# Row loads, one-hot global rows and eight-block units in a fused attention and feed-forward kernel

## The chip, the cores and the metric

The kernel runs on one core of one Trainium2 chip. The time of a run is the device time of that core in microseconds (us). A kernel is compared with another by runs taken on the same chip. The profiled span is a little shorter than the time of the same run (378.6 us of 380.3 before the change).

## The reference, cut to what matters

Eight batches of 576 tokens go through windowed attention with eight global tokens, and the 4,608 resulting rows of 512 go through a feed-forward layer with a snake activation.

```python
# attention: B=8, H=8, S=576, D=64; float32 inputs
mask = (abs(i - j) <= 32) | is_global[i] | is_global[j]
attn = softmax(where(mask, q @ k.T / sqrt(D), -1e9))
x = (attn @ v)            # to (B*S, H*D) = (4608, 512)
# feed-forward
h = x @ w_in              # (4608, 2048)
g = h + sin(alpha * h) ** 2 / (alpha + 1e-9)
out = g @ w_out           # (4608, 512), float32
```

The mask is sparse: a block of 48 queries sees 112 keys of its window and the 8 global keys. The 8 global query rows see every key; their sums are gathered over all blocks and written into their places at the end of a batch.

## The kernel before

The engines are PE (matmul), DVE and ACT (elementwise), POOL (elementwise, and the issuer of most loads) and SP (the issuer of plain copies and of the output). The order of instructions on each engine is the order in which the program is written. One batch of attention fills 576 columns of `xT`, and then one chunk of 512 tokens goes through the first matmul (`hb <- xT, w_in`). The second matmul of that chunk (`ops` and `o <- w_out, H2b`) is mixed into the next batch's attention. So PE runs a rhythm: a stretch of `hb` matmuls, then attention with second matmuls, then `hb` again. I call the time from one first `hb` matmul to the next a phase. The first matmul of a chunk is written in 16 steps of four `hb` matmuls, called slots (0 to 15); work of other kinds can be written between two of them.

The parts that the change touches:

```python
setup = tc.alloc_tile_pool(name="setup", bufs=1)
...
# q, k in tiles of 96 tokens; one DMA per head (batches 0, 1) or per tile (others)
QS = qkp.tile([TW, NTW, H, D], BF, name="QS")      # 96 x 6 x 8 x 64
...
# all 64 global rows of k, q, v, gathered at the start into tiles of their own
gN = [setup.tile([NG * B, DM], F32, name=f"gN{i}") for i in range(3)]
...                                                # registers loaded on SP and ACT
for i, src in enumerate((k, q, v)):
    for eng, js in halves:                         # half on SP, half on ACT
        for j in js:
            eng.dma_start(out=gN[i][j : NG * B : NG, :]..., in_=src[:, :, bass.ds(regs[j], 1), :]...)
nc.scalar.dma_start(out=alphaT[:], in_=moe_alpha.rearrange("(t p) -> p t", p=P))
...
def stage_T(b, hp, qpool, qtag):                   # 6 transposes of two heads each, for k and for q
    for jt in range(NTW):
        nc.tensor.transpose(out=Kps[:, WIN + jt * TW : ...], in_=KS[:, jt, 2 * hp : 2 * hp + 2, :], ...)
    nc.vector.tensor_copy(out=kTw[hp][:, :, 0:KB], in_=<overlapping windows of Kps>)
...
def stage_Q(psA, b, hp, hf):                       # one unit: 6 blocks
    ...                                            # 12 score matmuls
    nc.scalar.activation(out=E[:], in_=Sp[:, :, 0:EW], func=AF.Exp, scale=scale)
    nc.vector.tensor_tensor(out=E[:], in0=E[:], in1=mk..., op=ALU.mult)
...
def stage_V(psA, b, hp, hf, E, rec, gn):
    ...                                            # 12 matmuls num <- E, VW
    nc.vector.tensor_tensor(out=xT[:, hp, x0 : x0 + NU * QB]..., in0=num[:, :, 0:QB], in1=rec[:], op=ALU.mult)
...
def stage_G(b, gn, gr):                            # POOL scatters the global rows into xT
    for j in range(NG):
        nc.gpsimd.tensor_copy(out=xT[:, :, b * S : (b + 1) * S][:, :, bass.ds(pregs[j], 1)],
                              in_=xg[:, :, j : j + 1])
...
if p == 0:
    stage_T(0, 0, psA, "qp"); globals_all(); ...; globals_v_all()
    shift_v(0); global_v(0)                        # copies within the v buffer; global v rows into it
    parts, last = attention(0, psA, {2: 0, 3: 2})
    with_extra(parts, w_loads, 3, 2)               # 8 weight loads, two per part of the attention
    parts[3] = partial(chain, parts[3], pool_regs) # POOL loads 8 registers for the scatter
    late = load_slots(1, True)                     # batch 1 is loaded during chunk 0
```

The softmax here doesn't subtract the row's maximum and nothing guards it: scores larger than these inputs give would overflow.

## Time and profile before

| | before |
|---|---|
| time, median of 3 runs | 380.93 us (380.72 to 382.26) |
| profiled span | 378.6 us |
| first `hb` matmul | 46.60 us |
| first phase, second phase | 43.5 us, 38.1 us |
| each of the next five phases | 38.0 us |
| last `hb` start of a phase to the end | 60.4 us |

The page of the kernel before shows the span in 40 slices of 9.5 us; each digit is the busy share of a slice in tenths (`PEclk` is the granted TensorE clock in tenths):

```profile
span 378.6 us, 8594 instructions
...
PE   1127499698999999999999999999999999999996
...
DVE  7735459574987487748774877487748774866510
...
PEclk9999999999999999999999999999999999999999
DMA  6999999546999428951896289628962001000112
```

From slice 6 on PE is at 9 nearly everywhere. The opening, slices 1 to 5, is where PE has little to do, and there the DMA row is near full. `PEclk` reads 9 throughout, but the durations of the first `hb` matmuls say otherwise. The view of the line (shortest, median and longest duration in ns) shows those that ran between 46.6 and 49.6 us, and those between 50 and 52 us:

```profile
L457 PE MATMUL hb<-xT,w_in x7: 444/634/634, 46.6 to 49.5; 128*128 128x512 bf16 x7
...
L457 PE MATMUL hb<-xT,w_in x11: 379/379/380, 49.8 to 52.0; 128*128 128x512 bf16 x11
```

The first ones take 634 ns, the later ones 379. By these durations the kernel before starts its feed-forward at about half clock; its first eight `hb` matmuls (one of them is missing from the records) take 3.2 us.

The timeline of PE has start, duration, engine, line, operation and count, and in brackets what ended the idle time before:

```profile
29.58 0.57 PE L375 MATMUL num<-E,VW 128*64 128x56 bf16 x12 [3.08 <-DMA VW<-VgN]
...
46.60 0.59 PE L457 MATMUL hb<-xT,w_in 128*128 128x512 bf16 x1 [3.35 <-POOL xT L402]
```

The first product with v waited for the gathered global v rows until 29.58 us; the feed-forward started at 46.60 us, released by POOL's scatter into `xT`.

Two DMA views, 8 to 20 us and then 36 to 48 us, show what POOL's queue moved: packets, MB written, share of 16 engines.

```profile
q0 software_dynamic: 8487, 1.06, 139.0%
```

```profile
q0 software_dynamic: 2342, 2.32, 121.1%
```

In the first stretch the rows of q, k, v are 256 bytes, and 1.06 MB in 12 us is 88 GB/s; in the second the weights come in rows of 2 KB, and 2.32 MB in 12 us is 193 GB/s (bytes as written, in bf16), though the engines were no busier. The Trainium skill ("DMA: Bandwidth & Descriptors", Specifications) says that line rate needs transfers of at least 512 bytes; these two stretches agree with that.

The windows of the first three phases (columns named in the first line; busy us, with the number of instructions):

```profile
core 0: us, PE busy (x) PEld busy (x) DVE busy (x) ACT busy (x) POOL busy (x), PEclk, DMA share, GB/s
46.60:90.10 43.50, 37.92 (x378) 18.42 (x385) 28.59 (x73) 32.83 (x57) 23.85 (x44) 1.00 1.09 103
90.10:128.20 38.10, 36.95 (x378) 18.10 (x384) 26.89 (x64) 32.51 (x57) 31.40 (x53) 1.00 1.55 136
128.20:166.30 38.10, 36.38 (x379) 18.10 (x385) 26.64 (x59) 29.58 (x50) 31.24 (x48) 1.00 0.94 97
```

In the third window PE is busy for 36.38 of 38.10 us at full clock. A phase is bound by PE, and ACT or DVE time saved in it can gain little.

### The profile page before, as it was taken

The page shows a single profiled execution, that of the slowest core. Times are in us where ns is not written, and L with a number is a line of the kernel's source. Part 1 is how long each engine was busy: PE and PEld are TensorE (multiplying, and loading weights), DVE is VectorE, ACT ScalarE, POOL GpSimd, SP SyncE. Part 2 cuts the span into 40 slices and gives each one's busy share as a digit, 9 for nine tenths or more (in the row PEclk, how much of TensorE's full clock was granted, in tenths as well). Part 3 has the DMA queues.
Part 4 walks back from the last instruction along what each step waited for, and adds up shares of the span by engine and source line. Part 5 has one row for each costly group of instructions (what it writes and reads, how often), then busy time and mean ns, then how long its engine had stood idle before and what let it go on. Part 6 is the DMA issues. An engine that isn't in the chain of part 4 may idle for free.

```text
span 378.6 us, 8594 instructions
## 1 busy us (share of the span) xinstructions
PE 328.3 (87%) x3173; PEld 164.0 (43%) x3224; DVE 244.5 (65%) x556; ACT 258.1 (68%) x435; POOL 245.6 (65%) x390
## 2 busy tenths in 40 slices
PE   1127499698999999999999999999999999999996
PEld 0015244343444444444444444445444544444444
DVE  7735459574987487748774877487748774866510
ACT  1056587795998588858885888588858885845411
POOL 8944297136979489948994899489948303965100
PEclk9999999999999999999999999999999999999999
DMA  6999999546999428951896289628962001000112
GB/s 52 131 167 168 192 156 162 56 51 90 156 135 164 103 40 74 164 109 45 70 165 110 47 64 167 110 51 62 169 100 58 29 32 55 2 1 28 55 57 83
DMA packets 133867, 35.31 MB, mean 93 GB/s; under 512 B 123330, under 2 KB 128450, under 8 KB 133826
## 3 DMA queue, kind: packets, MB, share of 16 engines
q0 software_dynamic: 122560, 19.02, 70.0%
q1 hardware_dynamic: 8034, 15.40, 14.1%
q10 hardware_dynamic: 3232, 0.34, 0.8%
q8 instruction: 25, 0.41, 0.5%
q14 instruction: 16, 0.13, 0.1%
HBM read 38.42 MB, written 9.44 MB: 126 GB/s over the span
## 4 chain that ended last, share of the span: by engine, by line
PE 53%; ACT 17%; POOL 10%; issue 8%; DVE 8%; DMA 2%; POOLq 1%; ACTq 0%; DVEq 0%
PE hb L457 22%; PE ops L494 12%; PE o L494 8%; ACT Sb L464 6%; ACT E L342 3%; PE num L375 3%; ACT S L470 2%; DVE H2b L447 2%; DMA KS<-in_k_dram 2%; DVE S L472 2%; DVE kTw L310 2%; PE hb L494 2%; PE Sp L336 2%; ACT lnd L358 2%; POOL QS L95 2%
## 5 line engine op out<-in xcount | busy, mean ns | idle before, releaser
L457 PE MATMUL hb<-xT,w_in 128*128 128x512 bf16 x562 | 130.7, 382 | 7.0 <-POOL xT L402 4.8
L464 ACT ACTIVATE Sb<-hb,alphaT 128x512 bf16<-128x512 f32 x144 | 96.6, 684 | 52.4 <-PE hb L457 51.1
L447 DVE SCALAR_TENSOR_TENSOR H2b<-S,recipT,hb 128x512 bf16<-128x512 bf16 x144 | 102.2, 740 | 21.0 <-POOL S L472 21.0
L472 POOL TENSOR_TENSOR S<-Sb 128x512 bf16<-128x512 bf16 x87 | 88.4, 1040 | 29.7 <-ACT Sb L464 29.5
L457 PEld LDWEIGHTS <-w_in 128*128 128x128 bf16 x576 | 56.4, 98 | 73.7 <-issue 9.5
L494 PE MATMUL ops<-w_out,H2b 128*128 128x512 bf16 x286 | 73.3, 380 | 2.3 <-issue 1.7
L494 PEld LDWEIGHTS <-H2b 128*128 128x128 bf16 x560 | 48.7, 98 | 52.6 <-issue 2.2
L344 DVE TENSOR_TENSOR E<-E,MASK 128x672 bf16<-128x672 bf16 x64 | 33.1, 519 | 32.8 <-ACT E L342 32.1
L494 PE MATMUL o<-w_out,H2b 128*128 128x512 bf16 x206 | 50.6, 379 | 2.2 <-issue 1.9
L342 ACT ACTIVATE E<-Sp 128x672 bf16<-128x672 f32 x64 | 45.9, 717 | 4.1 <-PE Sp L336 4.0
L402 POOL COPY xT<-xg 128x4 bf16 x64 | 12.9, 201 | 48.7 <-DVE xg L400 45.3
L107 POOL DMA_DIRECT2D VW<-in_v_dram x56 | 42.7, 796 | 0.4 <-issue 0.3
L358 ACT ACTIVATE lnd<-den 128x288 f32<-128x288 f32 x64 | 26.4, 412 | 17.7 <-PE den L352 17.2
L472 DVE TENSOR_TENSOR S<-Sb 128x512 bf16<-128x512 bf16 x35 | 20.4, 582 | 25.0 <-ACT Sb L464 24.1
L382 DVE TENSOR_TENSOR xT<-num,rec 128x288 bf16<-128x288 f32 x64 | 28.7, 448 | 6.8 <-PE num L375 5.4
L375 PEld LDWEIGHTS <-VW 128*64 128x64 bf16 x768 | 18.3, 116 | 32.6 <-DVE gn L386 10.2
L375 PE MATMUL num<-E,VW 128*64 128x56 bf16 x768 | 25.3, 201 | 6.6 <-DMA VW<-VgN 3.1
L360 ACT ACTIVATE rec<-lnd 128x288 f32<-128x288 f32 x64 | 28.3, 443 | 2.0
L310 DVE COPY kTw<-Kps 128x1344 bf16<-128x1344 bf16 x32 | 27.1, 848 | 1.9 <-PE Kps L304 1.9
L336 PE MATMUL Sp<-qT,kTw 64*128 64x56 bf16 x768 | 22.1, 190 | 6.0 <-ACT E L342 4.2
L100 POOL DMA_DIRECT2D QS<-in_q_dram x30 | 23.6, 786 | 2.8 <-DMA QS<-in_q_dram 2.8
L324 ACT COPY qT<-qp 128x576 bf16<-128x576 bf16 x20 | 12.6, 632 | 18.1 <-DMA gN<-in_v_dram 13.7
(77 smaller groups left out, 314.3 us busy)
## 6 DMA issues: line engine op xcount, KB each, us to landing
out_dram<-osb SPq DMA_DIRECT2D x35, 256.0 KB
VW<-in_v_dram POOLq DMA_DIRECT2D x40, 112.0 KB, 4.4
VW<-VW SPq DMA_DIRECT2D x8, 384.0 KB
KS<-in_k_dram POOLq DMA_DIRECT2D x30, 96.0 KB, 4.6
QS<-in_q_dram POOLq DMA_DIRECT2D x30, 96.0 KB, 4.6
w_in<-in_moe_w_in_dram POOLq DMA_DIRECT2D x4, 512.0 KB, 9.0
w_out<-in_moe_w_out_dram POOLq DMA_DIRECT2D x4, 512.0 KB, 13.7
VW<-VW SPq DMA_DIRECT2D x8, 240.0 KB
```

The costliest lines, as they stand in the source:

```text
L107: nc.gpsimd.dma_start(out=W[p0 : p0 + n, par, u, :].rearrange("p (h d) -> p h d", d=D), in_=v[b, :, key0 : key0 + n, :].rearrange("h p d - ...
L310: nc.vector.tensor_copy(out=kTw[hp][:, :, 0:KB], in_=bass.AP(tensor=base.tensor, offset=base.offset, ap=[list(base.ap[0]), [QB, NW], [1, KB]],
L336: nc.tensor.matmul(out=Sp[:, t, u * QC : (u + 1) * QC], lhsT=kTw[hp][pr, i, :], rhs=qT[hp][pr, i, :], start=True, stop=True, skip_group_ch ...
L342: nc.scalar.activation(out=E[:], in_=Sp[:, :, 0:EW], func=AF.Exp, scale=scale)
L344: nc.vector.tensor_tensor(out=E[:], in0=E[:], in1=mk[:, None, :].to_broadcast([P, 2, EW]), op=ALU.mult)
L358: nc.scalar.activation(out=lnd[:], in_=den[:, :, 0:QB], func=AF.Ln)
L375: nc.tensor.matmul(out=num[pr, u, :], lhsT=W[:, i % 2, i // 2, c0 : c0 + 64], rhs=E[:, t, u * QC : (u + 1) * QC], start=True, stop=True, s ...
L447: nc.vector.scalar_tensor_tensor(out=H2b[:, n_, :], in0=s_[:], scalar=recipT[:, n_ : n_ + 1], in1=h_, op0=ALU.mult, op1=ALU.add,)
L457: nc.tensor.matmul(out=h2[:], lhsT=w_in[:, ci, nt * P : (nt + 1) * P], rhs=xT[:, ci, c * CH : (c + 1) * CH], start=(ci == 0), stop=(ci == ...
L464: nc.scalar.activation(out=Sb[:], in_=h2[:], func=AF.Sin, scale=alphaT[:, nt : nt + 1])
L472: eng.tensor_tensor(out=S2[:], in0=Sb[:], in1=Sb[:], op=ALU.mult)
L494: nc.tensor.matmul(out=ops[:], lhsT=H2b[:, nt, ts * P : (ts + 1) * P], rhs=w_out[:, nt, :], start=(nt == 0), stop=(nt == NT - 1),)
```

## The change

The intent is to shorten the opening and to relieve ACT and DVE. The changed parts are these:

1. q and k of batches 0 and 1 are loaded in rows of 8 tokens (2 KB contiguous), and transposed one head and one row position at a time.
2. Batch 0's mask is added by PE as a bias (identity times a bias tile) ahead of the scores; its global q and k rows come from matmuls with a one-hot tile (zeros with a single one in each column, so that the product picks out rows), its global v rows from eight small loads. So batch 0 no longer needs the big gather.
3. The big gather (24 transfers, all on SP now, after the v copies) lands in the last columns of `xT`, which are not used until the last batches; nothing else needs it before chunk 0.
4. A unit has 8 blocks rather than 6, so a batch has 6 units rather than 8.
5. The loads of POOL are written in one run (w_in, q and k of batch 1, w_out, v of batch 1), ahead of its register loads.
6. Batch 1 is transposed during chunk 0, and its global rows are converted there; the squares of the first two chunks go to POOL, as in the later ones.

```diff
+    late_x = slice(NTOK - 2 * DM, NTOK)
+    gN = [xT[0 : NG * B, i, late_x].bitcast(F32) for i in range(3)]
+    gB = [xT[0 : NG * B, 3, NTOK - (2 - i) * DM : NTOK - (1 - i) * DM] for i in range(2)]
...
+    def rows(src, dst, h0):                       # batches 0, 1
+        nc.gpsimd.dma_start(
+            out=dst[:, h0 : h0 + H // 2].rearrange("p h j d -> p h (j d)"),
+            in_=src[b, h0 : h0 + H // 2].rearrange("h (p j) d -> p h (j d)", j=R8))
...
+    VgF = setup.tile([P, DM], F32, name="VgF")
+    VgZ = setup.tile([P, DM], BF, name="VgZ")
+    zero(VgF[96:128, :])
+    nc.vector.memset(VgZ[:].bitcast(F32), 0.0)
+    ...                                           # per row: register load, then
+            eng.dma_start(out=VgF[KB + j : KB + j + 1, :]..., in_=v[0, :, bass.ds(regs[j], 1), :]...)
+    def gather_all():
+        for j in range(NG // 2, NG):
+            regs[j] = nc.sync.value_load(gsc[0:1, 2 * j : 2 * j + 1], min_val=0, max_val=S - 1)
+        nc.sync.dma_start(out=alphaT[:], in_=moe_alpha.rearrange("(t p) -> p t", p=P))
+        for i, src in enumerate((k, q, v)):
+            for j in range(NG):
+                nc.sync.dma_start(out=gN[i][j : NG * B : NG, :]..., in_=src[:, :, bass.ds(regs[j], 1), :]...)
...
     def globals_all():
         for i in range(2):
-            nc.vector.tensor_copy(out=gB[i][:], in_=gN[i][:])
+            nc.vector.tensor_copy(out=gB[i], in_=gN[i])
...
     def stage_T(b, hp, qpool, qtag):
+        if b < 2:
+            return stage_T8(b, hp, qpool, qtag)   # 16 transposes for k, 16 for q
+        if b == 2 and hp == 0:
+            zero(Kps[:, 0:WIN].bitcast(F32))
+            zero(Kps[:, WIN + S : WIN + S + WIN].bitcast(F32))
...
+        if b == 0:
+            for t, pr in heads:
+                nc.tensor.matmul(out=Sp[:, t, 0:EW], lhsT=identb[:], rhs=BIAS[...], start=True, stop=False, ...)
...
                 if p == 0:
                     stage_T(0, 0, psA, "qp")
-                    globals_all()
+                    globals_0(0, psC, "ops")      # one-hot matmuls
...
                     shift_v(0)
-                    global_v(0)
-                    parts, last = attention(0, psA, {2: 0, 3: 2})
-                    with_extra(parts, w_loads, 3, 2)
+                    gather_all()
+                    globals_v0()
+                    zero_v(1)
+                    parts, last = attention(0, psA, {2: -1, 3: 0})
+                    early = w_loads[:4] + load_rows(1) + w_loads[4:] + v_loads(1)
+                    chain(*early)
                     parts[3] = partial(chain, parts[3], pool_regs)
...
+                if p == 0:                        # during chunk 0
+                    gin = [partial(globals_in, 1, hp) for hp in range(NHP)]
+                    m1[8] = partial(chain, m1[8], globals_all, *gin)
```

## The prediction

> **What bounds the kernel now.** Span 378.6 us. (1) Opening: the first long run of expert matmuls starts at 47.41 us (chain of waits). The slices' DMA row is near full from about 2 to 48 us: 256-byte rows of q, k, v moved about 95 GB/s (DMA view, 8 to 20 us), the weights' 2 KB rows about 200 GB/s (36 to 48 us), counted as bf16. Batch 0 waits for the gathered global v rows until 29.6 us (timeline of PE), then runs its units; POOL's scatter ends at 46.6. (2) Steady phases of 38 us each (expert matmuls start at 128.9, 166.4, 204.9, 242.4, 280.9, 318.4): PE idles only 1 to 2 us in each (windows), so ACT or DVE savings gain little.
>
> **What the change does.** q and k of batches 0, 1 move in 2 KB rows: 1.18 MB per batch takes about 6 us of DMA instead of 12. Transposes grow from 12 to 32 per head pair; the kTw copy becomes strided (0.85 us, estimate 1.4). Batch 0 loses eight mask products (0.51 us each) and the wait for gathered v, and gains twelve bias matmuls and one-hot matmuls; its scores can start near 13 us instead of 20. Six units of eight blocks replace eight of six: ACT per batch 8 x (0.72+0.41+0.44) = 12.6 us becomes about 11.8; PE columns stay equal.
>
> **Where the gain should go.** Two new waits, read from the built program's order:
> - The gather's landing buffers now lie in xT. Batch 0's first product into xT waits for the last eight gather transfers, though nothing overlaps. SP issues all 24 after the v shift: start about 15 us, 24 x 0.8 us (measured), landing near 40. Five units and the sums remain: scatter done near 54.
> - POOL issues w_in, batch 1's q, k, w_out and batch 1's v before its register loads (5.3 us in the trace) and the scatter. An issue waits for the one eight earlier, so the last waits for the third w_out load: by bytes at the measured rates 44 to 46 us; plus registers and scatter, about 54.
>
> So expert matmuls start near 54 us instead of 47.4: plus 6 to 7. Given back: batch 1 is transposed during chunk 0's matmuls, and squares leave ACT; the 42.7 us to the next phase becomes about 40.5 (DVE has some 17 us of work in chunk 0): minus 2. Steady attention stretches (22.4 to 22.9 us) lose bubbles: minus 0.6 each, six times. Sum: about plus 1.
>
> The Trainium skill ("DMA: Bandwidth & Descriptors", opening table) puts line rate at transfers of 512 B and more; this case's rates, 95 against 200 GB/s, agree.
>
> **Prediction:** 382 us, 8 in 10 between 373 and 390. Faster by over 2%: 0.18; within 2%: 0.66; slower: 0.16.
>
> **What would show each step.** q, k landing near 6 us, v near 14. Scores of batch 0 before 15. DVE's first xT product idle until about 40, released by a gather DMA. POOL's register loads after 45; expert matmuls from 52 to 57. Next phase 40 to 41 us later; phases after that 37 to 38.
>
> **What would make it wrong.** Gathers issued or landed much faster, or the loads draining by 38 us: expert matmuls then come before 47, time near 372. Or 8-block units bound by ACT (1.96 us a unit against PE's 1.8), phases grow: near 388. Or one-head transposes costing PE several us in batch 1.

## The result, and the profile after

| | before | after |
|---|---|---|
| time, median | 380.91 us (4 runs) | 409.13 us (408.86 to 409.72, 4 runs) |
| profiled span | 378.6 us | 407.9 us |
| first `hb` matmul | 46.60 us | 71.00 us |
| first phase | 43.5 us | 45.0 us |
| second phase | 38.1 us | 42.2 us |
| next five phases together | 190.0 us | 189.8 us |
| rest | 60.4 us | 59.9 us |

The ratio of the times is 1.0735, with a 95% interval from 1.0707 to 1.0763. Here and below a ratio is the mean time of one kernel's fast runs over that of the other's fast runs of the same rounds, so it is not quite the ratio of the medians quoted. The kernel is slower, and outside the predicted range. By the rows of the table, the 29.3 us of span come from the opening (+24.4), the first phase (+1.5), the second phase (+4.0), the five steady phases (-0.2) and the end (-0.5).

The same rows of the page, after the change (slices of 10.2 us):

```profile
span 407.9 us, 9090 instructions
...
PE   2272025889897999999999999999999999999996
...
DVE  8330034578647664876497469638864975584530
...
PEclk9997558889998999999999999999999999999999
DMA  9999960009940795199409934972995000100022
```

Slices 4 to 6 of PE read 2, 0 and 2, and DVE's 0, 0 and 3: a hole from about 33 to 58 us, at whose end the DMA row runs out too. `PEclk` falls to 5 in the hole and is not back at 9 until slice 10, and it dips again to 8 in slice 13, near 130 us.

PE's timeline, at the places where it waited:

```profile
58.91 0.63 PE L516 MATMUL num<-E,VW 112*64 112x56 bf16 x16 [25.89 <-DVE gd L482]
...
71.00 9.28 PE L614 MATMUL hb<-xT,w_in 128*128 128x512 bf16 x36 [3.40 <-POOL xT L561]
82.16 0.29 PE L322 MATMUL ops<-identb,xT 64*128 64x64 bf16 x4 [1.88 <-DVE xT L320]
83.33 0.29 PE L322 MATMUL ops<-identb,xT 64*128 64x64 bf16 x4 [0.89 <-DVE xT L320]
...
116.01 9.66 PE L614 MATMUL hb<-xT,w_in 128*128 128x512 bf16 x44
128.70 0.64 PE L413 MATMUL Kps<-identb,KS 96*128 96x96 bf16 x6 [3.03 <-DVE Kps L184]
```

The hole of 25.89 us ends at 58.91 and is put down to DVE. The two waits of 1.88 and 0.89 us are for casts of the gathered rows, and the 3.03 us wait is for a zeroing of `Kps`. On DVE's timeline:

```profile
57.85 0.56 DVE L545 TENSOR_TENSOR xT<-num,rec 128x384 bf16<-128x384 f32 x1 [27.64 <-DMA xT<-in_v_dram]
...
81.52 1.75 DVE L320 CAST xT<-xT 64x512 bf16<-64x512 f32 x2
...
128.42 0.22 DVE L184 MEMSET Kps<- 128x16 f32 x2
```

DVE's first product into `xT`, ready since about 30 us, sat 27.64 us until a DMA into `xT` released it. The transfer named, `xT<-in_v_dram`, is one of the gathers; batch 0 writes the first 576 columns of `xT`, the gathers the last 1,024. Nothing overlaps. The prediction had read this wait from the built program's order.

SP issues the gathers. Its timeline shows what it did when; the view by line gives shortest, median and longest duration of the issues in ns:

```profile
10.22 7.54 SPq L296 DMA_DIRECT2D VgF<-in_v_dram  x4
18.02 0.57 SPq L140 DMA_DIRECT2D VW<-VW  x1
...
22.39 0.44 SPq L309 DMA_DIRECT2D alphaT<-in_moe_alpha_dram  x1
23.05 16.19 SPq L312 DMA_DIRECT2D xT<-in_k_dram  x8
39.43 6.72 SPq L312 DMA_DIRECT2D xT<-in_q_dram  x8
46.34 6.68 SPq L312 DMA_DIRECT2D xT<-in_v_dram  x8
```

```profile
L312 SPq DMA_DIRECT2D xT<-in_k_dram x8: 592/596/6982, 23.1 to 38.6; - x8
```

SP's one-row v loads (`VgF`) began at 10.22 us, after DVE had zeroed their tile, and ended at 17.76. The v copies went out at 18.02 and 18.65, four register loads took until 22.39, and then came the load of alpha. The k gathers right behind it took 16.19 us for eight issues, against 6.72 and 6.68 us for the q and v gathers. The issue right behind the alpha load took 6,982 ns, where their median is 596. The last k gather (38.65 us) came just after alpha's landing, at 22.39 + 16.24 = 38.63 us, as the chain of waits shows. In the kernel before, alpha came behind ACT's gathers, at 16.42 us, and held only a reciprocal on DVE. The chain:

```profile
22.39 16.24 DMA alphaT<-in_moe_alpha_dram
...
52.42 4.81 DMA xT<-in_v_dram
...
71.00 3.25 PE hb L614 x8
...
116.15 9.52 PE hb L614 x44
```

The second line of that chain is the last gather, issued at about 52.4 us and landed 4.8 us later. After the release at 57.85 us it took 13.2 us to the first `hb` matmul at 71.00. Those first eight took 3.25 us, 406 ns each; the 44 of the next phase took 9.52 us, 216 ns each.

POOL's scatter shows that POOL was not what held the opening, since it waited 20.36 us for DVE:

```profile
68.91 2.03 POOL L561 COPY xT<-xg 128x4 bf16 x8 [20.36 <-DVE xg L559]
```

Last, five windows after the change, with the columns as in the windows of before (the clock is the column after POOL's):

```profile
33.00:58.00 25.00, 0.01 (x2) 0.00 (x0) 0.15 (x1) 0.64 (x1) 5.38 (x7) 0.56 1.30 145
63.50:70.00 6.50, 2.76 (x77) 1.61 (x77) 3.63 (x14) 4.64 (x7) 0.85 (x5) 1.00 0.02 4
71.00:74.30 3.30, 3.30 (x10) 1.20 (x10) 0.00 (x0) 0.72 (x2) 0.63 (x1) 0.58 0.00 0
128.70:133.80 5.10, 5.10 (x37) 2.88 (x37) 2.52 (x4) 2.27 (x4) 1.40 (x2) 0.70 0.00 0
158.20:196.20 38.00, 36.67 (x382) 17.99 (x381) 26.10 (x51) 28.74 (x44) 30.94 (x48) 1.00 0.94 97
```

PE was granted 0.56 of its clock in the hole, 1.00 again from 63.5 to 70.0 us, 0.58 over the first `hb` matmuls, and 0.70 after the 3.03 us wait. So the low clock of the first `hb` matmuls came with the 3.40 us wait for the scatter just before them, not with the long hole. The Trainium skill ("TensorE: Matmul & The Clock Gate", "Why this matters for your kernels") warns of idle gaps beyond some 3 us, after which the clock is halved, and Part 1 gives 3.4 us of work before it is full again. Both agree: 406 ns a matmul after 3.40 us of waiting and 216 ns later, and the lower clock after 3.03 us of waiting. The eight slow matmuls are no loss against the kernel before, which has them too. The steady phase in the last line is no shorter than before (PE 36.67 us busy).

### The profile page after: what moved, and what is told of

Same layout as the page of the kernel before. It is cut to its first block, busy times and chain, and to the rows that moved or that the text cites. A ratio compares the mean times of both kernels' runs of the same rounds, so it can differ in the third digit from the quotient of the medians.

```text
span 407.9 us, 9090 instructions
## 1 busy us (share of the span) xinstructions
PE 340.5 (83%) x3508; PEld 168.6 (41%) x3508; DVE 238.3 (58%) x483; ACT 245.8 (60%) x373; POOL 250.7 (61%) x384
## 3 DMA queue, kind: packets, MB, share of 16 engines
q1 hardware_dynamic: 10922, 15.52, 14.4%
## 4 chain that ended last, share of the span: by engine, by line
PE 59%; ACT 12%; DMA 9%; DVE 8%; issue 5%; POOL 4%; SPq 2%; POOLq 0%; ACTq 0%; DVEq 0%
PE hb L614 26%; PE ops L651 12%; PE o L651 10%; DMA alphaT<-in_moe_alpha_dram 4%; ACT E L470 4%; PE num L516 3%; ACT Sb L621 3%; DVE S L629 2%; DVE H2b L604 2%; DVE kTw L419 2%; PE Sp L464 2%; ACT L578 2%; DMA w_in<-in_moe_w_in_dram 2%; DMA xT<-in_q_dram 2%; PE hb L651 2%
## 5 line engine op out<-in xcount | busy, mean ns | idle before, releaser
L629 POOL TENSOR_TENSOR S<-Sb 128x512 bf16<-128x512 bf16 x113 | 115.0, 1041 | 43.3 <-ACT Sb L621 42.9
L503 ACT ACTIVATE lnd<-den 128x384 f32<-128x384 f32 x48 | 23.5, 490 | 48.1 <-PE den L497 48.1
L561 POOL COPY xT<-xg 128x4 bf16 x64 | 12.9, 201 | 60.2 <-DVE xg L559 56.8
L470 ACT ACTIVATE E<-Sp 128x896 bf16<-128x896 f32 x48 | 43.6, 909 | 6.9 <-PE Sp L464 6.7
L516 PE MATMUL num<-E,VW 120*64 120x56 bf16 (+1 forms) x768 | 21.6, 198 | 27.2 <-DVE gd L482 25.9
L474 DVE TENSOR_TENSOR E<-E,MASK 128x896 bf16<-128x896 bf16 x42 | 26.4, 628 | 26.8 <-ACT E L470 26.7
L545 DVE TENSOR_TENSOR xT<-num,rec 128x384 bf16<-128x384 f32 x32 | 17.7, 554 | 30.7 <-DMA xT<-in_v_dram 27.6
L516 PEld LDWEIGHTS <-VW 120*64 120x64 bf16 (+1 forms) x768 | 16.5, 114 | 45.9 <-issue 38.5
L131 POOL DMA_DIRECT2D KS<-in_k_dram x36 | 28.2, 783 | 0.0
L505 ACT ACTIVATE rec<-lnd 128x384 f32<-128x384 f32 x48 | 25.1, 523 | 1.5
L629 DVE TENSOR_TENSOR S<-Sb 128x512 bf16<-128x512 bf16 x23 | 16.2, 703 | 16.1 <-ACT Sb L621 15.9
L464 PEld LDWEIGHTS <-kTw 64*128 64x128 bf16 x768 | 15.4, 95 | 23.2 <-issue 17.0
```

Source lines behind the costliest of these rows:

```text
L131: nc.gpsimd.dma_start(out=dst[:, t, :, :], in_=src[b, :, t * TW : (t + 1) * TW, :].rearrange("h p d -> p h d"),)
L464: nc.tensor.matmul(out=Sp[:, t, m * QC : (m + 1) * QC], lhsT=kTw[hp][pr, i, :], rhs=qT[hp][pr, i, :], start=b > 0, stop=True, skip_group_c ...
L474: nc.vector.tensor_tensor(out=E[:], in0=E[:], in1=mk[:, None, :].to_broadcast([P, 2, EW]), op=ALU.mult)
L505: nc.scalar.activation(out=rec[:], in_=lnd[:], func=AF.Exp, scale=-1.0)
L516: nc.tensor.matmul(out=num[pr, m, :], lhsT=W[0:nk, i % 2, i // 2, c0 : c0 + 64], rhs=E[0:nk, t, m * QC : (m + 1) * QC], start=b > 0 or m = ...
L629: eng.tensor_tensor(out=S2[:], in0=Sb[:], in1=Sb[:], op=ALU.mult)
```

## The experiments

The working theory, A, was that the time goes to the landing place: the gathers into `xT` hold DVE, and their lateness (alpha first, then register loads, one queue) sets how long. Rival B was that POOL's order of loads holds the start (its last v issue was at 48.03 us, and the register loads and the scatter stand behind it). Rival C was that the change makes PE's own work in the first two phases costlier, by transposes and the masks, whenever the start is. The runs were made on four chips; each ratio is to the kernel before on the same chip. All the outputs were correct. Every experiment is the changed kernel with the edits shown or named; from e9_mendv on, each builds on the one before it (e12_actcast on e10_best).

### e1_land: another landing place, all else the same

```diff
+    hpool = ctx.enter_context(tc.tile_pool(name="hpool", bufs=2))
-    gN = [xT[0 : NG * B, i, late_x].bitcast(F32) for i in range(3)]
+    gl = hpool.tile([P, NT, CH], BF, name="H2b")[0 : NG * B].rearrange("p t c -> p (t c)")
+    gN = [gl[:, 2 * i * DM : 2 * (i + 1) * DM].bitcast(F32) for i in range(3)]
```
(and `gB` likewise; the pool that holds H2b is made earlier)

> The changed kernel with the landing buffers of the global rows moved out of xT, into a buffer of H2b that stands free until later; nothing else moved. Theory A (batch 0's first product into xT waits for the gathers only because they land in xT): that product no longer waits for a DMA and runs near 30 us instead of 57.9; POOL's scatter is then held by POOL's own order (last v load of batch 1 issued near 48.6, register loads of 5.3 us): first expert matmul near 56 to 57 us instead of 71.0, time 393 to 396. Rival B (POOL's queue of DMA issues is what holds the scatter): no change, 408 to 410. Rival C (more transposes and a slower PE clock cost the time): at most 3 us gained.

Measured: 393.62 us, ratio 1.0305 [1.0284, 1.0325]. DVE's first product into `xT` in this run, and POOL's scatter:

```profile
30.19 0.56 DVE L546 TENSOR_TENSOR xT<-num,rec 128x384 bf16<-128x384 f32 x1 [0.17 <-PE num L527]
```

```profile
53.08 2.05 POOL L562 COPY xT<-xg 128x4 bf16 x8 [4.88 <-issue]
```

The product came at 30.19 us with the gathers as late as before; the wait of 27.64 us is gone, so the landing place made it. The start of `hb` moved from 71.00 only to 55.17 us, since now POOL's register loads (the 4.88 us ahead of the scatter, "issue") and the scatter behind the last v load set it. That is the second wait that the prediction named, at 55.17 for a predicted 54; after the change it was hidden behind the first one.

### e2_alpha: alpha's load early, on ACT's queue

```diff
     nc.scalar.dma_start(out=gcol[KB : KB + NG, :], in_=global_idx[:, None])
+    nc.scalar.dma_start(out=alphaT[:], in_=moe_alpha.rearrange("(t p) -> p t", p=P))
...
-        nc.sync.dma_start(out=alphaT[:], in_=moe_alpha.rearrange("(t p) -> p t", p=P))
```

> The changed kernel with only the load of alpha moved from SP, where the gathers queue behind it, to the front of ACT's queue. Theory A with its detail (eight gathers later the semaphore of the slow 4-byte-element load of alpha comes round, so the k gathers take 16.2 us instead of 6.2): the gathers land near 48 instead of 57.6, first expert matmul near 61, time 398 to 401. If the gathers are slow in themselves because the loads crowd the DMA engines: under 3 us gained.

Measured: 402.91 us, ratio 1.0525 [1.0502, 1.0547]. SP's gathers of k and q, and DVE's first product:

```profile
22.48 6.25 SPq L312 DMA_DIRECT2D xT<-in_k_dram  x8
28.91 9.23 SPq L312 DMA_DIRECT2D xT<-in_q_dram  x8
```

```profile
50.88 0.56 DVE L545 TENSOR_TENSOR xT<-num,rec 128x384 bf16<-128x384 f32 x1 [20.69 <-DMA xT<-in_v_dram]
```

The k gathers took 6.25 us in place of 16.19, so the alpha load cost 9.9 us there. DVE was released at 50.88, 7.0 us earlier, and `hb` started at 64.07, 6.9 us earlier. The start was expected near 61. The q gathers now took 9.23 us rather than 6.72: SP waited for slots among the k gathers instead, 2.7 us in five waits. And the last gather, issued at 43.78 us, released DVE 7.1 us later, where it had been 5.4. The packets of the alpha load can be counted: between the two pages, the queue of SP (q1) loses 2,064 packets (10,922 to 8,858) and another one (q10) gains 2,064 (368 to 2,432).

### e3_pool: POOL's order, all else the same

```diff
-                    early = w_loads[:4] + load_rows(1) + w_loads[4:] + v_loads(1)
+                    early = w_loads[:4] + load_rows(1) + [pool_regs] + w_loads[4:]
-                    parts[3] = partial(chain, parts[3], pool_regs)
...
+                    with_extra(m1, v_loads(1), 0, 1)     # during chunk 0
```

> The changed kernel with only POOL's order mended: register loads before the w_out loads, batch 1's v loads after the scatter, one behind each slot of chunk 0's matmuls. Theory A: the wait for the gathers still ends last, first expert matmul within 1.5 us of 71, time 407 to 411 (a little more if the later v loads delay POOL's squares or the shift of v). Rival B: first expert matmul at 50 to 57 us, time 390 to 396.

Measured: 410.86 us, ratio 1.0744 [1.0725, 1.0762], no gain in time. The start of `hb` was at 68.50, 2.5 us earlier and a little outside the 1.5 us expected, since DVE was released at 55.05 instead of 57.85. The first phase more than gave it back: 49.7 us rather than 45.0, with a wait of PE of 6.43 us for the casts of the gathered rows. POOL was free 33.88 us before the scatter and waited for DVE. So POOL's order was not what held the start in the changed kernel.

### e4_landpool: e1 and e3 together

> Both edits together (landing buffers out of xT, and POOL's order). Theory A with POOL's order as the second wait behind it: units of batch 0 run from 30 us, scatter near 43, first expert matmul near 44 us, but the global rows still land near 57 us, so their transposes in slot 8 of chunk 0 (about 52 us) stall PE some 5 us: time 383 to 390. If only the landing mattered: same as that edit alone.

The edit is those of e1_land and e3_pool. Measured: 389.49 us, ratio 1.0187 [1.0170, 1.0205]. PE's timeline:

```profile
44.78 0.58 PE L615 MATMUL hb<-xT,w_in 128*128 128x512 bf16 x1 [3.60 <-POOL xT L562]
...
60.88 0.39 PE L323 MATMUL ops<-identb,H2b 64*128 64x64 bf16 x4 [5.51 <-DVE H2b L321]
```

With both waits out of the way the feed-forward starts at 44.78 us, ahead of the 46.60 of the kernel before, so taking both waits away returns the opening's whole loss. But 5.7 of these 26.2 us were given back: the gathers had not landed when the casts of their rows came up in chunk 0, PE waited 5.51 us for them, and the first phase grew from 45.0 to 50.7 us.

### e6_kps: the zeroing of Kps earlier

```diff
-        if b == 2 and hp == 0:
-            zero(Kps[:, 0:WIN].bitcast(F32))
-            zero(Kps[:, WIN + S : WIN + S + WIN].bitcast(F32))
...
+                    if p == 1:                    # in batch 1's attention, where Kps is free
+                        parts[6] = partial(chain, parts[6], partial(zero, Kps[...]), partial(zero, Kps[...]))
```

> The changed kernel with only the two small memsets of the key buffer's edges for batch 2 moved from DVE's place in chunk 1's matmuls (behind its late H2b sums) to batch 1's attention, after its last key copy. If PE's stall of 3.0 us at 128.7 us, and the half-clock stretch after it, are what lengthens that phase (42.2 us against 38.0 in the phases after it): that phase becomes 38 to 38.5 and the time 404.5 to 406. If the phase is long for another reason (one-head rows, 8-block units): under 1 us gained.

Measured: 404.50 us, ratio 1.0606 [1.0582, 1.0630], which is 1.3 points of the ratio below the change as a whole (1.0735). The second phase went from 42.2 to 38.0 us. The whole of the second phase's loss was this one zeroing, two memsets of 0.22 us in all, queued on DVE behind work of the chunk while PE waited, with the lower clock after it. (The whole change was timed in another session, and so 4.6 us by the medians and 4.9 by the ratios are both fair readings.)

### e7_casts: the casts of the gathered rows ahead of chunk 0

```diff
     def globals_all():
         for i in range(2):
-            nc.vector.tensor_copy(out=gB[i], in_=gN[i])
...
+            if p == 0:
+                m1[0] = partial(chain, globals_cast, m1[0])
```

> The changed kernel with only the three casts of the gathered rows moved from slot 8 of chunk 0's matmuls to ahead of slot 0, where DVE idles; the transposes stay in slot 8. If PE's two stalls at 80.3 to 83.3 us (1.9 and 0.9 us) and the lower clock after them lengthen the first phase (45.1 us): it becomes 41 to 43 and the time 405.5 to 407.5. If DVE's total work sets that phase: no gain.

Measured: 404.96 us, ratio 1.0614 [1.0584, 1.0645]. The first phase went from 45.0 to 41.9 us. The waits of 1.88 and 0.89 us and the low clock behind them are gone. What is left against the 40.5 predicted is 1.4 us, but 0.8 of it is a difference of counting: the prediction took 42.7 us for the phase before, from the second `hb` matmul shown (47.41 us), where the table has 43.5, from the first (46.60). The other 0.6 us stays open. The eight `hb` matmuls at half clock don't account for it, since the kernel before has them as well. Rival C falls with this run and e6_kps: without the two waits, each in its own run, the first two phases are 41.9 (e7_casts) and 38.0 us (e6_kps), shorter than or equal to the 43.5 and 38.1 of before, with all the added transposes in them.

### e8_mend: all five edits together

The edits are those of e1_land, e2_alpha, e6_kps, the casts at slot 7 of chunk 0, and e3_pool's order with four of the v loads still ahead of the scatter:

```diff
+                    vl = v_loads(1)
+                    early = w_loads[:4] + load_rows(1) + [pool_regs] + w_loads[4:] + vl[:4]
...
+                m1[7] = partial(chain, globals_cast, m1[7])
...
+                    with_extra(m1, vl[4:], 1, 1)
```

> All five mends together (landing out of xT, alpha on ACT's queue, POOL's register loads early and only the last three v loads behind chunk 0's slots, key-edge memsets early, casts in slot 7 and transposes in slot 11). If the losses are the ones named and add up: first expert matmul at 45, first phase 40 to 42, second 38, five phases of 38 and 60 at the end: time 374 to 380, so the intent of the change is worth 1 to 6 us against before once its waits are gone. If something else in the change costs time (one-head transposes, bias matmuls): above 384.

Measured: 381.50 us, ratio 1.0015 [0.9991, 1.0040], a little above what was expected. The loss is gone but nothing is gained. The `hb` start was 45.53 us, as expected, and the second phase 38.0, but the first phase was 46.1 rather than 40 to 42. The trace shows two things there: POOL's squares and v loads alternated in chunk 0 (a square of 1.05 us and an issue of 0.86 to 0.89 us, so some 1.9 us a slot), and DVE's three casts, from 56.97 to 60.2 us, stood ahead of the sum for which PE waited 2.40 us. This run doesn't tell the two apart; e10_best and e12_actcast do in part.

### e9_mendv: e8 with the tile of the one-row v loads zeroed earlier, and alpha behind them on ACT

```diff
+    zero(VgF[96:128, :])
     zero_v(0)
+    nc.vector.memset(VgZ[:].bitcast(F32), 0.0)
     for f in v_loads(0) + kq0[2:]:
...
-    nc.scalar.dma_start(out=alphaT[:], ...)       # front of ACT's queue
+    nc.scalar.dma_start(out=alphaT[:], ...)       # behind ACT's one-row v loads
```

> The five mends, and the two memsets of the buffer for batch 0's gathered v moved to the front of DVE's order, so that SP and ACT issue those eight loads near 3 us instead of 10.2 (alpha after them). ACT's copy of the first queries then comes near 9 us instead of 18.5 and the first scores near 14; the first expert matmul then depends on the shift of v: 38 to 42 us instead of 45. Time 2 to 6 us below the five mends, 370 to 376. If the v shift binds already: within 1 us of the five mends.

Measured: 378.56 us, ratio 0.9927 [0.9902, 0.9952], 2.9 us below e8_mend. That is within the 2 to 6 us expected; the start, at 42.41 us, was a little later than the 38 to 42. Two lines say what held it. The first is from POOL's timeline, the second from SP's waits (in total, times, longest, us):

```profile
39.48 0.82 POOL L103 DMA_DIRECT2D VW<-in_v_dram  x1 [0.16 <-issue]
40.29 2.06 POOL L563 COPY xT<-xg 128x4 bf16 x8
```

```profile
SPq L314 <- DMA alphaT<-in_moe_alpha_dram: 11.1, 1, 11.1
```

DVE's sums were ready at 37.07 us, but POOL was issuing v loads and scattered at 40.29. And the alpha load, now amid the bulk loads, was slow again: 21.79 us from 11.10, and SP's gathers waited 11.1 us for it, although it had been issued from another engine. So another queue alone does not help; what e2_alpha has besides is that alpha goes before the bulk loads.

### e10_best and e11_best6: alpha first again, two v loads ahead of the scatter; and the same with six-block units

```diff
+    nc.scalar.dma_start(out=alphaT[:], ...)       # front of ACT's queue again
...
-                    early = ... + vl[:4]
+                    early = ... + vl[:2]
...
+    sq_first = lambda nt: {1: nc.vector, 2: nc.scalar, 3: nc.vector, 4: nc.scalar, ...}.get(nt, nc.gpsimd)
-                m1[7] = partial(chain, globals_cast, m1[7])
+                m1[8] = partial(chain, globals_cast, m1[8])
```
and for e11_best6 on top of it:
```diff
-    NB = 8
+    NB = 6
```
(with the counts and sums that depend on it; e10_best also moves SP's four register loads ahead of the v copies)

> A version meant to beat both kernels, after the trace of the mends with early v gathers (scatter held 3.2 us by POOL's issue of v loads, chunk 0's squares slowed to one in 1.86 us where POOL issues v loads between them, alpha landing after 21.8 us and holding the k gathers again, casts waiting for the last gathers). Alpha goes to the front of ACT's queue, SP's four register loads ahead of the v shift, only two v loads of batch 1 ahead of the scatter, five behind slots 1 to 5 of chunk 0, whose squares go to DVE and ACT; casts in slot 8, transposes in slot 12. If these waits are what is left: first expert matmul at 38 to 41 us, first phase 40 to 42.5, time 370 to 375, about 2% below before. If chunk 0's phase is bound by DVE's and POOL's total work in it: first phase 44 to 46 and time 375 to 379.

> The same with units of six blocks, eight to a batch, as before had them, so that only the unit size differs. If the 8-block units save what was predicted (0.6 us in each of seven phases): 3 to 5 us slower than the eight-block version. If steady phases are set by PE's own work, as their equal length in the traces of before and of the change says (37.9 and 38.0 us): within 2 us of it, phases of 37.5 to 38.5.

Measured: 376.80 us, ratio 0.9867 [0.9838, 0.9896], with eight blocks, and 377.08 us, ratio 0.9857 [0.9821, 0.9894], with six. The two cannot be told apart. The eight-block unit spares ACT 6.1 us of busy time (247.1 for 253.2) and DVE 7.0 us (240.1 for 247.1), and gives nothing that can be seen in the time. e10_best missed the expected 370 to 375 us. Its start was at 42.29, still behind POOL's v loads, and its first phase was 45.7: DVE was busy almost without a gap from 49.9 to 68 us, and its three casts (1.80 us for two and 1.25 us) held the sums that free PE's buffers, though the squares of slots 1 to 5 had left POOL, three of them for DVE.

### e12_actcast and e13_allv: e10 with the casts on ACT; and then all the v loads behind the scatter

```diff
-            nc.vector.tensor_copy(out=gB[i], in_=gN[i])
-        nc.vector.tensor_copy(out=VgN[:], in_=gN[2][:])
+            nc.scalar.copy(out=gB[i], in_=gN[i])
+        nc.scalar.copy(out=VgN[:], in_=gN[2][:])
```
and for e13_allv on top of it:
```diff
-                    early = ... + w_loads[4:] + vl[:2]
+                    early = ... + w_loads[4:]
-                    with_extra(m1, vl[2:], 1, 1)
+                    with_extra(m1, vl, 0, 1)
```

> The last eight-block version with one more edit: the three casts of the gathered rows go from DVE to ACT, at the same place. In its trace DVE works without a gap from 49.9 to 68 us of the first phase (45 us long against 38 for the later ones), 4.8 us of it in these casts. If DVE's total work sets that phase: first phase 41 to 43 us, time 373 to 375. If it is POOL's squares and v loads: within 1 us of 376.8.

> That version with, besides, all seven v loads of batch 1 behind POOL's scatter, one after each of the first seven slots of chunk 0. The scatter then waits only for DVE's sums (36.8 us in the trace before): first expert matmul at 39.5 instead of 43, but POOL's loads crowd its squares in two more slots. Theory (the scatter is held by POOL's order): 1 to 3 us below the version before it, 370 to 374. If the phase is bound by POOL's total work: no gain.

Measured: e12_actcast 373.91 us, ratio 0.9804 [0.9787, 0.9821]; its first phase was 42.4 us in place of 45.7. e13_allv 371.19 us, ratio 0.9722 [0.9701, 0.9742]. The scatter and PE's phase starts in e13_allv:

```profile
36.57 0.73 POOL L561 COPY xT<-xg 128x4 bf16 x3 [3.25 <-DVE xg L559]
```

```profile
38.86 0.59 PE L614 MATMUL hb<-xT,w_in 128*128 128x512 bf16 x1 [3.61 <-POOL xT L561]
...
81.79 9.66 PE L614 MATMUL hb<-xT,w_in 128*128 128x512 bf16 x43
```

Both runs came out as expected. The scatter now follows DVE's sums directly, `hb` starts at 38.86 us, 7.7 us before the kernel before, and the first phase is 42.9 us. This version beats both kernels: 2.8% less time than before by the ratio. It keeps what the change computes; landing place, order, and the engine of the casts and of some squares differ. Whether the kernel before would gain from the same mends (alpha first, other engines for the squares) was not tried.

## Why the prediction was wrong

**The step that failed: "landing near 40".** The mechanism was foreseen: "Batch 0's first product into xT waits for the last eight gather transfers, though nothing overlaps". The size was not. The last gather landed at 57.2 us (52.42 + 4.81), 17 us later than said, and `hb` started at 71.0 rather than "near 54". The term was built as 15 + 24 x 0.8 us plus a landing. The runs show in its place: the v copies went out at 18.0 rather than 15, because SP had been in the one-row v loads from 10.2 to 17.8; four register loads followed, which the sum left out (to 22.4); the alpha load made the k gathers take 16.2 us rather than 6.3 (e2_alpha gave back 6.9 us of start by it alone); and the last issue at about 52.4 landed 4.8 us later. The issue cost itself was right, about 0.8 us a gather. What had been left out was that the alpha load is an obstacle on SP's queue. In all, the prediction's sum was about plus 1 us, and the span grew by 29.3. By its own terms the difference is 17.9 us in the opening (24.4 for 6.5), 3.5 in the first phase (plus 1.5 for minus 2), 4.0 in the second, 3.4 of bubbles that did not come back, and minus 0.5 at the end. The Trainium skill ("DMA: Bandwidth & Descriptors", "Rules for kernel authors") says that a transfer with a strided last dimension becomes one descriptor per element; alpha is 128 x 16 elements laid out that way, so 2,048 elements of 4 bytes. 2,064 packets change queues with it (e2_alpha), and it took 16.24 us to land amid the loads, 21.79 us in e9_mendv. That the count of descriptors is the reason was not tested by itself.

**The time after the release** was right: five units, the sums, the scatter took 13.2 us, where the prediction had about 14.

**POOL's order** was right as a second wait, predicted at about 54 and found at 55.17 in e1_land, but in the changed kernel it lay hidden behind the first. Taking it away alone gained nothing (e3_pool); taking both away put `hb` at 44.78 (e4_landpool).

**The first phase**, "about 40.5", was 45.0. DVE did have work to do, but the prediction did not see that the casts for the global rows stood where PE needed them (2.8 us of waits, then a low clock). e7_casts brought it to 41.9; of the 1.4 us left, 0.8 is the other start of counting, and 0.6 stays open.

**The second phase**, "37 to 38", was 42.2. The one cause is the zeroing of `Kps` for batch 2, which the prediction did not mention: 3.03 us of wait and then matmuls at 0.70 of the clock. e6_kps brought it to 38.0.

**"Steady attention stretches lose bubbles: minus 0.6 each, six times"** did not happen. The five steady phases took 189.8 us for 190.0. The busy time of ACT did fall, from 258.1 to 245.8 us, and DVE's from 244.5 to 238.3 (all parts of the change together), but these phases are bound by PE, and e11_best6 shows no difference between six and eight blocks.

**What was right besides:** the transposes of one head cost PE no several us (first two phases with the waits removed: 41.9 and 38.0 us), and the units of eight were not bound by ACT. The idea of a shorter opening can be had as well: e13_allv, where the waits are out of the way, starts `hb` 7.7 us earlier than the kernel before, with mends of its own besides.

**Two signs named in the prediction did not show:** the scores of batch 0 came at 20.7 us rather than before 15, since ACT issued its four of the one-row v loads from 10.22 to 18.47 and only then copied q (18.52; 11.03 in e10_best, where these loads come earlier); and the v copies went out at 18.0 rather than near 15. The first had no cost here, since DVE's long wait came after it; the second is 3 us of the gathers' late start.

What stays open: how much the one queue (24 gathers on SP, where the kernel before had 12 each on SP and ACT) and the register loads cost by themselves, since only alpha was moved alone; why the issue right behind the alpha load takes 7 us; and which DMA exactly POOL's and SP's later issues wait for, since the view of waits infers it. The experiments settle that these waits follow the alpha load's place, not how they come about inside.

## What to carry to other kernels

If a buffer is borrowed as a landing place, every later writer of that buffer may have to wait for the landing, even if the parts are disjoint, so borrow one that nobody touches until the data is needed. When a prediction rests on when transfers land, add up the issuing engine's whole list from the trace (memsets it waits for, register loads, slow small loads), not the transfers alone. A wait that is taken away uncovers the next one: look at the start of the bound stage after each edit, and remove waits in the order in which they end last.

## What the Trainium skill lacked or had wrong

- No page has it: in the program as built, a transfer into one part of a tile held a write by DVE into another, disjoint part of the same tile, 27.64 us; with another landing place the same instruction came at 30.19 rather than 57.85 us (e1_land). Whether the whole tile is held, or the view of it in another type, was not tested.
- "DMA: Bandwidth & Descriptors" tells of strided loads that they become one descriptor per element, but gives no figure for what they cost the issues behind them: the next issue took 6.98 us, where the median is 0.60, and the eight gathers behind it 16.19 us rather than 6.25 (e2_alpha); a load from ACT's queue held SP's issues 11.1 us (e9_mendv).
- The same page, "Issuing engines are not separate DMA queues", calls the time to initiate a DMA usually small beside the transfer. It was small here for a single transfer (0.59 us for the last gather, which landed 4.81 us after its issue began), but it adds up and can decide a start: 24 gathers went out one after the other, some 0.8 us each, and POOL's v loads held its scatter 3.2 us (e9_mendv, 37.07 to 40.29).
- "TensorE: Matmul & The Clock Gate" agrees: 406 ns a matmul of 128x512 after a wait of 3.40 us, 216 ns later; after a wait of 3.03 us the clock was 0.70 over the next 5 us.
